# The cross terms of a complex filter product formed on VectorE, with one inverse matmul per class

## The chip, the cores and the metric

One Trainium2 chip, one of its eight NeuronCores. The metric is the device time of one execution of the whole program in microseconds (us), the median of the executions that were timed. A ratio of two kernels is computed as the mean time of one kernel's runs over that of the other's runs of the same rounds, so it is not quite the ratio of the medians that are quoted.

## The reference, cut to what matters

```python
def _attn_ref(x, filt_r, filt_i):            # x: 8 x 3008 x 256
    X = np.fft.rfft(x, axis=1)
    Y = X * (filt_r + 1j * filt_i)[None]     # complex product, one filter for all batches
    return np.fft.irfft(Y, n=x.shape[1], axis=1).astype(np.float32)

def _moe_ref(x, w_in, w_out, alpha):         # x: 24064 x 256, hidden width 2048
    h = x @ w_in
    s = np.sin(alpha * h)
    return ((h + s * s / (alpha + 1e-09)) @ w_out).astype(np.float32)
```

The kernel computes the Fourier transforms as matmuls in three stages per batch. Stage 1 is a 47-point transform. Stage 2 has 12 units of two frequency classes each: a forward matmul by the twiddle table, the product with the filter, and an inverse matmul. Stage 3 is the inverse 47-point transform. Between the stages the data go through DRAM to change the layout. The result feeds the "snake" layer: hidden matmuls (`ph`), a cosine on ScalarE, one VectorE instruction that makes `v`, and projection matmuls (`po`). The stages of the next batch are woven into the steps of the snake layer; one step is two hidden tiles and about eight projection matmuls, 48 steps are one batch.

## The kernel before

This is stage 2, as code. `xf` holds the spectrum with the real part in partitions 0 to 63 and the imaginary part in 64 to 127. `f_t[0]` and `f_t[1]` hold the real and the imaginary filter, each copied into both halves.

```python
        def stage2(u):
            if u < 12:
                ps = ...                                   # PSUM
                for i in range(2):
                    nc.tensor.matmul(out=ps[:, i, :], lhsT=d_t[:, s, :], rhs=..., ...)   # pb: forward
                xf = xfpool.tile([128, 2, C], FP16, ...)
                nc.scalar.copy(out=xf, in_=ps)
                for k in range(2):                         # two products of 128 x 512
                    nc.vector.tensor_tensor(out=pt, in0=xf, in1=f_t[k][:, 2 * u:2 * u + 2, :], op=ALU.mult)
            if u > 0:
                w = u - 1
                for i in range(2):
                    for k in range(2):                     # pc: two inverse matmuls per class add them up
                        nc.tensor.matmul(out=ps[:, i, :], lhsT=e_t[:, k, 2 * w + i, :],
                                         rhs=pr[k][:, i, :], start=(k == 0), stop=(k == 1))
                evac(st["g"][:, i0:i0 + 2, :], ps, ...)    # to g, then by DMA to DRAM (d2)
```

Because the second inverse matmul uses a table `e_t[:, 1]` with swapped and negated halves, TensorE forms the cross terms and their sum by accumulating in PSUM. The rest that the argument touches is the weaving:

```python
    def evac(dst, src, on_act=None):            # PSUM evacuations: every third on VectorE
        flip[0] = (flip[0] + 1) % 3
        ...
    hps = pool("hps", 4, PSUM)                  # four buffers for hidden tiles
    ...
    plan = {1: [-45 + i for i in range(8)],     # steps, counted from the first step that needs the batch
            2: [-29 + 14 * i / 13 for i in range(13)],
            3: [-10, -9] + [-7 + 2 * i for i in range(14)]}
```

Stage 2 therefore takes 14 of the 48 steps of a batch. The compiler's scheduler decides the exact order of each engine's instructions; the argument takes it that each engine keeps to that order at run time. TensorE's weight loads run beside its matmuls (544.2 and 799.8 us busy in a span of 837.2 us).

Of the kernel before, what the change touches and what calls it, by code (L numbers as in the profile page):

```python
# [9 lines left out]
FP16 = mybir.dt.float16  # L10
FP32 = mybir.dt.float32
AFT = mybir.ActivationFunctionType
ALU = mybir.AluOpType
# [3 lines left out]
B, S, C = 8, 3008, 256  # L17
DFF = 2048
N1, N2 = 47, 64
NS, NQ = 24, 64  # L20
# [34 lines left out]
def kernel(  # L55
# [10 lines left out]
    nc = tc.nc  # L66
# [17 lines left out]
    def pool(name, bufs, space=None):  # L84
        kw = {} if space is None else {"space": space}
        return ctx.enter_context(tc.tile_pool(name=name, bufs=bufs, **kw))
# [3 lines left out]
    t1pool = pool("t1", 4)  # L90
    t2pool = pool("t2", 4)
    xfpool = pool("xf", 3)
    ppool = pool("pp", 4)
    gpool = pool("gp", 4)
    t4pool = pool("t4", 3)
    opool = pool("op", 3)
# [3 lines left out]
    fps = pool("fps", 2, PSUM)  # L100
    hps = pool("hps", 4, PSUM)
    ops = pool("ops", 2, PSUM)
# [4 lines left out]
    d_t = cpool.tile([128, NS, 128], FP16)  # L107
    e_t = cpool.tile([128, 2, NS, 128], FP16)
    wi_t = cpool.tile([NK, NR], FP16)
    f_t = [cpool.tile([128, NS, C], FP16, name=f"filt{i}") for i in range(2)]  # L110

    marks = {}
# [17 lines left out]
    flip = [0]  # L130

    def evac(dst, src, on_act=None):
        flip[0] = (flip[0] + 1) % 3
        if flip[0] if on_act is None else on_act:
            marks["act"] = nc.scalar.copy(out=dst, in_=src)  # L135
        else:
            marks["dve"] = nc.vector.tensor_copy(out=dst, in_=src)  # L137

    def spectral(b):

        pieces = []
        d1 = dpool.tile([2 * NS, N2, C], FP16, name=f"d1_{b}", tag="d1")
        d2 = dpool.tile([2 * NS, N2, C], FP16, name=f"d2_{b}", tag="d2")
        d1_rows = d1.rearrange("a (h n) c -> (a h) n c", h=2)
        d2_rows = d2.rearrange("a (h n) c -> (a h) n c", h=2)
        st = {}

        def stage1(u):
            ch, half = divmod(u, 2)
            if u == 0:  # L150
                st["x"] = load_x(b)
            if half == 0:
                st["t1"] = t1pool.tile([NK, 8, C], FP16, name=f"t1_{b}_{ch}", tag="t1")
            for i in range(2):
                n0 = 4 * half + 2 * i
                ps = fps.tile([128, 512], FP32, name=f"pa_{b}_{u}_{i}", tag="f")
                marks["pe"] = nc.tensor.matmul(out=ps[0:NK, :], lhsT=wf_t, rhs=st["x"][ch][:, n0:n0 + 2, :],  # L157
                                               start=True, stop=True)
                evac(st["t1"][:, n0:n0 + 2, :], ps[0:NK, :])
            if half == 1:  # L160
                nc.sync.dma_start(out=d1_rows[:, 8 * ch:8 * ch + 8, :], in_=st["t1"])
            if u == 7:
                st["t2"] = []
                for g in range(4):
                    t2 = t2pool.tile([128, 6, C], FP16, name=f"t2_{b}_{g}", tag="t2")
                    for p in range(2):
                        a0 = p * NS + 6 * g
                        eng = nc.scalar if b == 0 and p else nc.sync
                        marks["t2", g] = eng.dma_start(out=t2[64 * p:64 * p + 64, :, :],
                                          in_=d1[a0:a0 + 6, :, :].rearrange("s n c -> n s c"))  # L170
                    st["t2"].append(t2)

        def stage2(u):
            if u < 12:

                ps = (ops if b == 0 else fps).tile([128, 2, C], FP32, name=f"pb_{b}_{u}",
                                                   tag="o" if b == 0 else "f")
                for i in range(2):
                    s = 2 * u + i
                    nc.tensor.matmul(out=ps[:, i, :], lhsT=d_t[:, s, :],  # L180
                                     rhs=st["t2"][s // 6][:, s % 6, :], start=True, stop=True)
                xf = xfpool.tile([128, 2, C], FP16, name=f"xf_{b}_{u}", tag="xf")
                nc.scalar.copy(out=xf, in_=ps)  # L183
                pr = []
                for k in range(2):
                    pt = ppool.tile([128, 2, C], FP16, name=f"p_{b}_{u}_{k}", tag="p")
                    marks["prod", u] = nc.vector.tensor_tensor(out=pt, in0=xf, in1=f_t[k][:, 2 * u:2 * u + 2, :],  # L187
                                                               op=ALU.mult)
                    pr.append(pt)
                st["p", u] = pr  # L190
            if u > 0:
                w = u - 1
                pr = st.pop(("p", w))
                if w % 3 == 0:
                    st["g"] = gpool.tile([128, 6, C], FP16, name=f"g_{b}_{w}", tag="g")
                ps = fps.tile([128, 2, C], FP32, name=f"pc_{b}_{w}", tag="f")
                for i in range(2):
                    for k in range(2):
                        nc.tensor.matmul(out=ps[:, i, :], lhsT=e_t[:, k, 2 * w + i, :],  # L199
                                         rhs=pr[k][:, i, :], start=(k == 0), stop=(k == 1))  # L200
                i0 = 2 * (w % 3)
                evac(st["g"][:, i0:i0 + 2, :], ps, i0 != 2 if b == 0 else None)
                if w % 3 == 2:
                    for p in range(2):
                        a0 = p * NS + 6 * (w // 3)
                        nc.sync.dma_start(out=d2[a0:a0 + 6, :, :].rearrange("s n c -> n s c"),
                                          in_=st["g"][64 * p:64 * p + 64, :, :])

        def stage3(u):
            ch, rest = divmod(u, 4)  # L210
            half, cb = divmod(rest, 2)
            if rest == 0:
                t4 = t4pool.tile([NK, 8, C], FP16, name=f"t4_{b}_{ch}", tag="t4")
                marks["t4"] = nc.sync.dma_start(out=t4, in_=d2_rows[:, 8 * ch:8 * ch + 8, :])
                st["t4"] = t4
            ps = fps.tile([128, 4, 128], FP32, name=f"pd_{b}_{u}", tag="f")
            psv = ps.rearrange("p a b -> p (a b)")[:, 0:4 * NR].rearrange("p (a r) -> p a r", r=NR)
            for i in range(4):
                nc.tensor.matmul(out=psv[:, i, :],  # L219
                                 lhsT=st["t4"][:, 4 * half + i, cb * 128:cb * 128 + 128],  # L220
                                 rhs=wi_t, start=True, stop=True)
            n0 = 8 * ch + 4 * half
            evac(y[:, cb, b % 2, n0:n0 + 4, :], psv)

        for u in range(8):
            pieces.append((1, lambda u=u: stage1(u)))
        for u in range(13):
            pieces.append((2, lambda u=u: stage2(u)))
        for u in range(16):
            pieces.append((3, lambda u=u: stage3(u)))  # L230
        return pieces
# [24 lines left out]
    for i in range(2):  # L256
        al_row.append(opool.tile([128, 2, C], FP32, name=f"al_row_{i}", tag="o"))
        for h in range(2):
            nc.scalar.dma_start(
                out=al_row[i][64 * h:64 * h + 1].rearrange("p a b -> p (a b)"),  # L260
# [3 lines left out]

    def dup_filter(g):
        gs = slice(6 * g, 6 * g + 6)
        for k in range(2):
            ins = nc.vector.tensor_copy(out=f_t[k][64:128, gs, :], in_=f_t[k][0:64, gs, :])
            behind(ins, marks["prod", 3 * g - 2] if g else s1_dve)

    for g in range(4):
# [9 lines left out]
    for g in range(3):  # L281
        pse = ops.tile([128, 8, 128], FP16, name=f"pse_{g}", tag="o")
        for i in range(8):
            behind(nc.tensor.transpose(out=pse[:, i, :], in_=d_t[:, 8 * g + i, :], identity=id16),
                   s1_pe)
        gs = slice(8 * g, 8 * g + 8)
        behind(nc.scalar.mul(e_t[:, 0, gs, :], pse, 0.125), s1_act)
        nc.vector.tensor_copy(out=e_t[0:64, 1, gs, :], in_=e_t[64:128, 0, gs, :])
        nc.vector.tensor_scalar(out=e_t[64:128, 1, gs, :], in0=e_t[0:64, 0, gs, :],
                                scalar1=-1.0, scalar2=None, op0=ALU.mult)  # L290

    ones = cpool.tile([128, 128], FP32)
    nc.vector.memset(ones, 2.0)
# [85 lines left out]
    def store(o_blk, pb, col):  # L379

        p = 0
        while p < 128:
# [11 lines left out]


    plan = {1: [-45 + i for i in range(8)],
            2: [-29 + 14 * i / 13 for i in range(13)],
            3: [-10, -9] + [-7 + 2 * i for i in range(14)]}
    pending = [(1 + i % 4 + 8 * (i // 4), 0, piece) for i, (_, piece) in enumerate(first[25:])]
    for b in range(1, B):  # L400
        at = {1: 0, 2: 0, 3: 0}
        for stage, piece in spectral(b):
            at_step = 48 * b + plan[stage][at[stage]]
            if b == 1 and stage < 3:
                at_step = 8 + at[stage] if stage == 1 else 23 + at[stage]
            at[stage] += 1
            pending.append((at_step, b, piece))
    pending.sort(key=lambda p: p[0])
# [46 lines left out]
```

## Time and profile before

| | before |
|---|---|
| time | 840.77 us, median of 3 (839.44 to 841.71) |
| TensorE (PE) busy | 96% |
| VectorE (DVE) busy | 75% |
| ScalarE (ACT) busy | 73% |
| GpSimd (POOL) busy | 3% |

The first part of the profile's page of the kernel before, the busy time of each engine in us, its share of the span and its instructions:

```profile
PE 799.8 (96%) x5793; PEld 544.2 (65%) x5793; DVE 628.1 (75%) x1119; ACT 613.0 (73%) x1200; POOL 28.3 (3%) x55
```

Two groups of instructions of the kernel before: line, engine, operation, output and inputs, shape, count, then busy us and mean ns of one, then the idle time of the engine ahead of them.

```profile
L187 DVE TENSOR_TENSOR p<-xf,filt 128x512 f16<-128x512 f16 x192 | 72.1, 419 | 4.9 <-ACT xf L183 4.5
...
L199 PE MATMUL pc<-p,e_t 128*128 128x256 f16 x384 | 59.7, 275 | 2.6 <-DVE p L187 1.5
```

Both means are latencies, not rates: instructions of one engine overlap. Rates are read from start to start. Here is stage 2 of batch 4 of the kernel before, first as busy time by stretch (us, busy us and instructions of PE, weight loads, DVE, ACT, POOL, then the granted clock of TensorE, the share of the DMA engines, and GB/s), then as VectorE's timeline (start, us, what, count, and the idle time ahead of it):

```profile
core 0: us, PE busy (x) PEld busy (x) DVE busy (x) ACT busy (x) POOL busy (x), PEclk, DMA share, GB/s
393.00:422.00 29.00, 28.95 (x214) 20.73 (x213) 25.27 (x52) 24.03 (x48) 0.00 (x0) 1.00 0.31 72
```

```profile
19.17 0.42 DVE L288 COPY e_t<-e_t 64x1024 f16<-64x1024 f16 x1
19.61 0.42 DVE L289 TENSOR_SCALAR e_t<-e_t 64x1024 f16<-64x1024 f16 x1
20.08 0.42 DVE L288 COPY e_t<-e_t 64x1024 f16<-64x1024 f16 x1
...
399.07 0.76 DVE L187 TENSOR_TENSOR p<-xf,filt 128x512 f16<-128x512 f16 x2
400.26 1.28 DVE L358 SCALAR_TENSOR_TENSOR v<-cos,ph 128x512 f16<-128x512 f32 x2 [0.43 <-ACT cos L357]
401.46 0.76 DVE L187 TENSOR_TENSOR p<-xf,filt 128x512 f16<-128x512 f16 x2
402.13 0.68 DVE L137 CAST g<-pc 128x512 f16<-128x512 f32 x1
402.73 1.28 DVE L358 SCALAR_TENSOR_TENSOR v<-cos,ph 128x512 f16<-128x512 f32 x2
```

What to see: TensorE has no gap in stage 2 (28.95 of 29 us), and VectorE has little room left (25.27 of 29). Two products take 0.75 us and one 0.42, so the second starts 0.335 us after the first. A snake instruction costs 0.60 (two take 1.28, one 0.68). The three lines at 19 to 20 us are set-up work whose input and output change partition halves from one instruction to the next: they start 0.44 and 0.47 us apart and do not overlap at all, though each lasts only 0.42.

### The profile page before, as it was taken

The numbers are of one execution on the slowest core, as the hardware profiler recorded it, in microseconds if no ns is written. First come the engines' busy times: TensorE is split into PE (matmuls) and PEld (weight loads), VectorE is DVE, ScalarE is ACT, GpSimd is POOL, SyncE is SP. The second block draws the span as 40 slices with busy tenths as digits, with TensorE's granted clock in tenths as the row PEclk, the third lists the DMA queues.
The fourth block names the chain that finished last, engine by engine and source line by source line (L and its number), as shares of the span: only waits on it lengthen the run. The fifth ranks groups of instructions, "written<-read, shape, count | busy, mean of one in ns | idle before, by whom it ended". The sixth has DMA issues, their size and how long they took to land.

```text
span 837.2 us, 16122 instructions
## 1 busy us (share of the span) xinstructions
PE 799.8 (96%) x5793; PEld 544.2 (65%) x5793; DVE 628.1 (75%) x1119; ACT 613.0 (73%) x1200; POOL 28.3 (3%) x55
## 2 busy tenths in 40 slices
PE   5758999999999999999999999999999999999996
PEld 2425676667776677666776677666777677666674
DVE  3658886778877788777877788777877778777772
ACT  4536886787868787787877777777877878677763
POOL 3210000000000000000000000000000000000000
PEclk9969999999999999999999999999999999999999
DMA  9985835185344744266242763447443353421111
GB/s 220 218 255 117 200 89 130 51 174 116 82 135 81 171 99 109 75 141 153 65 130 60 165 137 82 115 91 171 92 96 94 97 113 83 115 58 38 38 40 45
DMA packets 93495, 94.98 MB, mean 113 GB/s; under 512 B 8084, under 2 KB 82852, under 8 KB 93416
## 3 DMA queue, kind: packets, MB, share of 16 engines
q1 hardware_dynamic: 84784, 75.02, 34.5%
q0 software_dynamic: 6704, 18.09, 12.5%
q10 hardware_dynamic: 1928, 0.86, 0.5%
q8 instruction: 45, 0.74, 0.3%
q14 instruction: 34, 0.28, 0.1%
HBM read 58.02 MB, written 49.81 MB: 129 GB/s over the span
## 4 chain that ended last, share of the span: by engine, by line
PE 83%; DMA 7%; ACT 4%; issue 3%; DVE 2%; POOL 0%; SPq 0%; ACTq 0%; DVEq 0%; POOLq 0%
PE po L369 36%; PE ph L354 35%; PE pc L199 4%; PE pa L157 3%; ACT cos L357 2%; PE pd L219 2%; PE pb L180 2%; DMA t<-d 1%; DMA w_out<-in_moe_w_out_dram 1%; DMA d<-g 1%; DMA d_t<-d_tbl 1%; DVE p L187 1%; DMA x<-in_x_dram 1%; DMA filt<-in_filt_i_dram 1%; ACT t L135 1%
## 5 line engine op out<-in xcount | busy, mean ns | idle before, releaser
L358 DVE SCALAR_TENSOR_TENSOR v<-cos,ph 128x512 f16<-128x512 f32 (+1 forms) x768 | 484.0, 672 | 164.0 <-ACT cos L357 163.5
L357 ACT ACTIVATE cos<-ph 128x512 f32<-128x512 f32 (+1 forms) x768 | 411.6, 589 | 153.9 <-PE ph L354 152.5
L369 PE MATMUL po<-w,v 128*128 128x256 f16 x3008 | 400.9, 273 | 2.6 <-DVE w L337 2.6
L354 PE MATMUL ph<-y,w 128*128 128x512 f16 (+1 forms) x1536 | 391.5, 377 | 0.2 <-ACT y L135 0.2
L369 PEld LDWEIGHTS <-v 128*128 128x128 f16 x3008 | 289.0, 98 | 80.9 <-issue 8.7
L354 PEld LDWEIGHTS <-w 128*128 128x128 f16 x1536 | 150.4, 98 | 101.0 <-issue 4.6
L187 DVE TENSOR_TENSOR p<-xf,filt 128x512 f16<-128x512 f16 x192 | 72.1, 419 | 4.9 <-ACT xf L183 4.5
L375 ACT COPY o<-po 128x512 f32<-128x512 f32 x96 | 55.6, 579 | 17.7 <-PE po L369 15.5
L135 ACT CAST t<-pa 96x512 f16<-96x512 f32 x89 | 51.0, 589 | 19.0 <-PE pa L157 18.9
L183 ACT CAST xf<-pb 128x512 f16<-128x512 f32 x96 | 57.0, 595 | 8.1 <-PE pb L180 5.5
L219 PEld LDWEIGHTS <-t 96*128 96x128 f16 x512 | 36.3, 100 | 39.8 <-DMA t<-d 11.8
L199 PE MATMUL pc<-p,e_t 128*128 128x256 f16 x384 | 59.7, 275 | 2.6 <-DVE p L187 1.5
L157 PE MATMUL pa<-x,wf_t 94*96 94x512 f16 x128 | 47.2, 408 | 10.1 <-DMA x<-in_x_dram 6.3
L219 PE MATMUL pd<-wi_t,t 96*128 96x94 f16 x512 | 43.4, 208 | 11.1 <-DMA t<-d 10.9
L135 ACT CAST y<-pd 128x376 f16<-128x376 f32 x82 | 39.1, 479 | 12.5 <-PE pd L219 12.5
L199 PEld LDWEIGHTS <-e_t 128*128 128x128 f16 x384 | 37.6, 99 | 15.6 <-issue 7.1
L180 PE MATMUL pb<-t,d_t 128*128 128x256 f16 x192 | 38.2, 283 | 2.5 <-DMA t<-d 1.5
L135 ACT CAST g<-pc 128x512 f16<-128x512 f32 x64 | 38.7, 605 | 1.6 <-PE pc L199 1.6
L137 DVE CAST t<-pa 96x512 f16<-96x512 f32 x39 | 26.6, 683 | 15.8 <-PE pa L157 15.8
L180 PEld LDWEIGHTS <-d_t 128*128 128x128 f16 x192 | 18.9, 101 | 23.8 <-issue 4.6
L118 POOL DMA_DIRECT2D x<-in_x_dram x32 | 16.7, 524 | 502.8 <-PE pa L157 490.5
L157 PEld LDWEIGHTS <-wf_t 94*96 94x96 f16 x128 | 16.6, 129 | 19.6 <-issue 9.9
(28 smaller groups left out, 94.3 us busy)
## 6 DMA issues: line engine op xcount, KB each, us to landing
d<-t SPq DMA_DIRECT2D x32, 384.0 KB
d<-g SPq DMA_DIRECT2D x64, 192.0 KB
t<-d SPq DMA_DIRECT2D x32, 384.0 KB
x<-in_x_dram POOLq DMA_DIRECT2D x32, 376.0 KB, 6.9
t<-d SPq DMA_DIRECT2D x60, 192.0 KB
out_dram<-o SPq DMA_DIRECT2D x72, 94.0 KB
w_in<-in_moe_w_in_dram POOLq DMA_DIRECT2D x2, 1024.0 KB, 9.2
w_out<-in_moe_w_out_dram POOLq DMA_DIRECT2D x1, 2048.0 KB, 11.6
```

The lines of the kernel that those rows point to most:

```text
L135: marks["act"] = nc.scalar.copy(out=dst, in_=src)
L157: marks["pe"] = nc.tensor.matmul(out=ps[0:NK, :], lhsT=wf_t, rhs=st["x"][ch][:, n0:n0 + 2, :], start=True, stop=True)
L180: nc.tensor.matmul(out=ps[:, i, :], lhsT=d_t[:, s, :], rhs=st["t2"][s // 6][:, s % 6, :], start=True, stop=True)
L183: nc.scalar.copy(out=xf, in_=ps)
L187: marks["prod", u] = nc.vector.tensor_tensor(out=pt, in0=xf, in1=f_t[k][:, 2 * u:2 * u + 2, :], op=ALU.mult)
L199: nc.tensor.matmul(out=ps[:, i, :], lhsT=e_t[:, k, 2 * w + i, :], rhs=pr[k][:, i, :], start=(k == 0), stop=(k == 1))
L219: nc.tensor.matmul(out=psv[:, i, :], lhsT=st["t4"][:, 4 * half + i, cb * 128:cb * 128 + 128], rhs=wi_t, start=True, stop=True)
L354: nc.tensor.matmul(out=ps[:, 0:n], lhsT=w1[:, cb, jb * 128:jb * 128 + 128], rhs=y_cols[:, cb, c0:c0 + n], start=(cb == 0), stop=(cb == 1))
L357: nc.scalar.activation(out=cs[:, 0:n], in_=ps[:, 0:n], func=AFT.Sin, bias=float(np.pi / 2))
L358: marks["snake"] = nc.vector.scalar_tensor_tensor(out=v[k][:, jb, 0:n], in0=cs[:, 0:n], scalar=-1.0, in1=ps[:, 0:n], op0=ALU.add, op1=ALU. ...
L369: nc.tensor.matmul(out=pso[k][:, t % 2, :], lhsT=v[k][:, jb, 128 * t:128 * t + 128], rhs=w2[:, jb, :], start=(jb == 0), stop=(jb == 15))
L375: nc.scalar.copy(out=o[:, 0:nb, :], in_=pso[k][:, 0:nb, :])
```

## The change

The intent is to take matmuls off TensorE, which limits the kernel. From batch 1 on VectorE forms the cross terms itself: two half products read one partition half and write the other one, a full product gives the direct terms, and an add folds both into one tile ("the fold" from here on). One inverse matmul per class is then enough. The sign moves into the filter's upper half. Evacuations move from VectorE to ScalarE (one in five instead of one in three), and stage 2 gets a 14th piece, because the inverse matmul now comes one piece later.

```diff
-    ppool = pool("pp", 4)
+    ppool = pool("pp", 6)
...
-        flip[0] = (flip[0] + 1) % 3
+        flip[0] = (flip[0] + 1) % 5
...
+        lo, hi, every = slice(0, 64), slice(64, 128), slice(0, 128)
...
         def stage2(u):
             if u < 12:
+                forward(u)
+            if 0 <= u - 1 < 12:
+                new_products(u - 1)
+                prod(nc.vector, 1, u - 1, lo, hi)       # reads 0..63, writes 64..127
+                prod(nc.vector, 1, u - 1, hi, lo)       # reads 64..127, writes 0..63
+                prod(nc.vector, 0, u - 1, every, every)
+            w = u - 1
+            if 0 <= w < 12:
+                p0, p1 = st["p", w]
+                nc.vector.tensor_tensor(out=p0, in0=p0, in1=p1, op=ALU.add)
+                st["p", w].pop()
+            if 0 <= w - 1 < 12:
+                inverse(w - 1)                          # one matmul per class
...
-            2: [-29 + 14 * i / 13 for i in range(13)],
+            2: [-30 + 14 * i / 13 for i in range(14)],
```

Batch 0 keeps the old form (`stage2_first`, cut here, as are the filter's sign and the table's).

More of the change, by code (lines that the diff above doesn't have):

```diff
@@ L171, in stage1, with forward @@
                     st["t2"].append(t2)
+        def forward(u):
+            ps = (ops if b == 0 else fps).tile([128, 2, C], FP32, name=f"pb_{b}_{u}",
+                                               tag="o" if b == 0 else "f")
+            for i in range(2):
+                s = 2 * u + i
+                nc.tensor.matmul(out=ps[:, i, :], lhsT=d_t[:, s, :],
+                                 rhs=st["t2"][s // 6][:, s % 6, :], start=True, stop=True)
+            xf = xfpool.tile([128, 2, C], FP16, name=f"xf_{b}_{u}", tag="xf")
+            nc.scalar.copy(out=xf, in_=ps)
+            st["xf", u] = xf
@@ new lines, in inverse @@
+        def inverse(w):
+            pr = st.pop(("p", w))
+            if w % 3 == 0:
+                st["g"] = gpool.tile([128, 6, C], FP16, name=f"g_{b}_{w}", tag="g")
+            ps = fps.tile([128, 2, C], FP32, name=f"pc_{b}_{w}", tag="f")
+            for i in range(2):
+                for k, pt in enumerate(pr):
+                    nc.tensor.matmul(out=ps[:, i, :], lhsT=e_t[:, k, 2 * w + i, :],
+                                     rhs=pt[:, i, :], start=(k == 0), stop=(k == len(pr) - 1))
+            i0 = 2 * (w % 3)
+            evac(st["g"][:, i0:i0 + 2, :], ps, i0 != 2 if b == 0 else None)
+            if w % 3 == 2:
+                for p in range(2):
+                    a0 = p * NS + 6 * (w // 3)
+                    nc.sync.dma_start(out=d2[a0:a0 + 6, :, :].rearrange("s n c -> n s c"),
+                                      in_=st["g"][64 * p:64 * p + 64, :, :])
@@ new lines, in prod, with new_products, stage2_first @@
+        def prod(eng, k, u, rows, to):
+            marks["prod", u] = eng.tensor_tensor(out=st["p", u][k][to, :, :], in0=st["xf", u][rows, :, :],
+                                                 in1=f_t[k][rows, 2 * u:2 * u + 2, :], op=ALU.mult)
+        def new_products(u):
+            st["p", u] = [ppool.tile([128, 2, C], FP16, name=f"p_{b}_{u}_{k}", tag="p") for k in range(2)]
+        lo, hi, every = slice(0, 64), slice(64, 128), slice(0, 128)
+        def stage2_first(u):
+            if u < 12:
+                forward(u)
+                new_products(u)
+                for k in range(2):
+                    prod(nc.vector, k, u, every, every)
+            if u > 0:
+                inverse(u - 1)
@@ L173, in stage2 @@
         def stage2(u):
             if u < 12:
-                ps = (ops if b == 0 else fps).tile([128, 2, C], FP32, name=f"pb_{b}_{u}",
-                                                   tag="o" if b == 0 else "f")
-                for i in range(2):
-                    s = 2 * u + i
-                    nc.tensor.matmul(out=ps[:, i, :], lhsT=d_t[:, s, :],
-                                     rhs=st["t2"][s // 6][:, s % 6, :], start=True, stop=True)
-                xf = xfpool.tile([128, 2, C], FP16, name=f"xf_{b}_{u}", tag="xf")
@@ L183, in stage2 @@
-                nc.scalar.copy(out=xf, in_=ps)
-                pr = []
-                for k in range(2):
-                    pt = ppool.tile([128, 2, C], FP16, name=f"p_{b}_{u}_{k}", tag="p")
-                    marks["prod", u] = nc.vector.tensor_tensor(out=pt, in0=xf, in1=f_t[k][:, 2 * u:2 * u + 2, :],
-                                                               op=ALU.mult)
-                    pr.append(pt)
-                st["p", u] = pr
-            if u > 0:
-                w = u - 1
-                pr = st.pop(("p", w))
-                if w % 3 == 0:
-                    st["g"] = gpool.tile([128, 6, C], FP16, name=f"g_{b}_{w}", tag="g")
-                ps = fps.tile([128, 2, C], FP32, name=f"pc_{b}_{w}", tag="f")
-                for i in range(2):
-                    for k in range(2):
-                        nc.tensor.matmul(out=ps[:, i, :], lhsT=e_t[:, k, 2 * w + i, :],
-                                         rhs=pr[k][:, i, :], start=(k == 0), stop=(k == 1))
-                i0 = 2 * (w % 3)
-                evac(st["g"][:, i0:i0 + 2, :], ps, i0 != 2 if b == 0 else None)
-                if w % 3 == 2:
-                    for p in range(2):
-                        a0 = p * NS + 6 * (w // 3)
-                        nc.sync.dma_start(out=d2[a0:a0 + 6, :, :].rearrange("s n c -> n s c"),
-                                          in_=st["g"][64 * p:64 * p + 64, :, :])
@@ new lines, in stage2 @@
+                forward(u)
+            if 0 <= u - 1 < 12:
[10 more added lines that the diff above has]
+                inverse(w - 1)
@@ L226, in spectral @@
             pieces.append((1, lambda u=u: stage1(u)))
-        for u in range(13):
-            pieces.append((2, lambda u=u: stage2(u)))
+        for u in range(13 if b == 0 else 14):
+            pieces.append((2, lambda u=u: (stage2_first if b == 0 else stage2)(u)))
         for u in range(16):
@@ L266, in dup_filter @@
         gs = slice(6 * g, 6 * g + 6)
-        for k in range(2):
-            ins = nc.vector.tensor_copy(out=f_t[k][64:128, gs, :], in_=f_t[k][0:64, gs, :])
+        for ins in (nc.vector.tensor_copy(out=f_t[0][64:128, gs, :], in_=f_t[0][0:64, gs, :]),
+                    nc.vector.tensor_scalar(out=f_t[1][64:128, gs, :], in0=f_t[1][0:64, gs, :],
+                                            scalar1=-1.0, scalar2=None, op0=ALU.mult)):
             behind(ins, marks["prod", 3 * g - 2] if g else s1_dve)
@@ L288 @@
         nc.vector.tensor_copy(out=e_t[0:64, 1, gs, :], in_=e_t[64:128, 0, gs, :])
-        nc.vector.tensor_scalar(out=e_t[64:128, 1, gs, :], in0=e_t[0:64, 0, gs, :],
-                                scalar1=-1.0, scalar2=None, op0=ALU.mult)
+        nc.vector.tensor_copy(out=e_t[64:128, 1, gs, :], in_=e_t[0:64, 0, gs, :])
     ones = cpool.tile([128, 128], FP32)
@@ L404 @@
             if b == 1 and stage < 3:
-                at_step = 8 + at[stage] if stage == 1 else 23 + at[stage]
+                at_step = 8 + at[stage] if stage == 1 else 23 + 13 * at[stage] / 13
             at[stage] += 1
```

## The prediction

> **What bounds the kernel now.** TensorE. The page gives it 96% busy (799.8 of 837.2 us), and from about 80 us on it is busy 99.7 of every 100 us (busy time by stretch). VectorE is 75% and ScalarE 73% busy, but unevenly. In stage 2 of a later batch (392 to 422 us, by the timeline) one unit takes about 2.4 us of TensorE: four hidden matmuls, two forward, four inverse, eight projections. In the same stretch VectorE has idle gaps of only about 0.45 us per unit, and none where it also evacuates a `g` tile. So VectorE is already close to full there.
>
> **Removed.** Batches 1 to 7 lose 2 of 4 inverse matmuls in 12 units: 168 matmuls. Eight 256-column matmuls start 0.87 us after the eight before, so one costs 0.109 us (the group table's mean of 275 ns is latency). That is 168 x 0.109 = 18.3 us, all of it on the critical path: 2.2%. Alone it would give 822 us.
>
> **Added.** Per unit, VectorE goes from two 128x512 products to two half-partition products, one full product and one add. In the trace two products in a row take 0.75 us, one takes 0.42, so they start 0.335 apart. A half product has as many elements per partition, so it costs as much. The Trainium skill ("VectorE: DVE Perf Modes", section "Two Vector instructions with no wait between them") says that an instruction whose input or output starts in another partition quadrant than the last one's starts only when all earlier ones have finished. The trace agrees: the filter copy into the upper half starts after the product in front has ended, and the `e_t` copies (0.42 us each, alternating halves) start 0.44 us apart with no overlap. So each half product costs about 0.45 us, and the instruction ahead of the first loses its overlap of 0.1 us: 0.10 + 0.45 + 0.45 + 0.335 + 0.335 = 1.67 us per unit, against 0.67. The evacuations that move to ScalarE (1 in 5 instead of 1 in 3) give back 0.08.
>
> **On the critical path.** I counted the compiled instruction order. Between a batch's first product and last add VectorE has 48 products and adds, 25 to 27 snake operations (0.60 apart) and 2 or 3 evacuations: 36 to 38 us. TensorE's work for the same steps is 27 to 29 us. VectorE becomes the limit of stage 2, by about 9 us per batch, 63 us in seven. Lag can hide part: four hidden PSUM buffers and the later place of the inverse matmuls let TensorE lead by about a step, an estimated 2 us per batch, 14 in all. Net: 840.8 - 18.3 + 63 - 14 = 871; I take 869. Outside stage 2 nothing much changes; batch 0 is as before.
>
> **What would show it.** Product and add group: about 0.42 us each; half products without overlap. VectorE over 95% busy in each stage 2, no longer waiting for ScalarE there. TensorE busy about 80% there instead of 100%, its waits on PSUM freed by VectorE and on the add. Stage 2 about 36 us instead of 29. Inverse matmuls 216, not 384. Time outside stage 2 unchanged.
>
> **What would make it wrong.** If half products overlap (no hold), stage 2 needs 4 us less per batch, and the result is about 840. If buffers hide more of the lag, the loss shrinks. If TensorE's and VectorE's in-order waits interlock, it grows. Faster needs both no hold and nearly full hiding.
>
> Predicted 869 us, range 846 to 888; faster by over 2%: 0.04; within 2%: 0.15; slower by over 2%: 0.81.

## The result, and the profile after

The changed kernel takes 875.09 us, median of 4 (872.24 to 878.00), against 840.61 us for the kernel before in the same rounds: ratio 1.0411, 95% interval 1.0373 to 1.0448. It is slower by 4%, inside the predicted range of 846 to 888 and 6 us above the predicted 869. The profile is of the slowest of the four (878.0 us).

| | before | after |
|---|---|---|
| time, us | 840.61 | 875.09 |
| inverse matmuls | 384 | 216 |
| VectorE products and adds | 192 | 360 |
| span of a later batch's products and adds on VectorE, us | 27.3 to 29.1 | 36.6 to 38.2 |
| mean granted clock of TensorE | 0.988 | 0.979 |

Part 1 of the page of the changed kernel, and its groups that answer to those of before, shapes kept apart:

```profile
PE 802.2 (92%) x5625; PEld 526.1 (60%) x5625; DVE 673.6 (77%) x1242; ACT 638.0 (73%) x1245; POOL 28.1 (3%) x55
```

```profile
L203 DVE TENSOR_TENSOR p<-xf,filt 64x512 f16<-64x512 f16 x168 | 70.5, 420 | 4.4 <-ACT xf L182 0.5
...
L192 PE MATMUL pc<-p,e_t 128*128 128x256 f16 x216 | 42.1, 283 | 16.9 <-DVE p L233 12.2 <-DVE p L203 1.5 <-DVE g L137 1.1
...
L233 DVE TENSOR_TENSOR p<-p,p 128x512 f16<-128x512 f16 x84 | 35.2, 419 | 0.2
```

A half product takes 420 ns, the same as a full one. On average over the span VectorE looks harmless at 77%. The stretches tell more. Here are stage 2 of batch 4 and three slices of 2 us after the end of stage 2 of batch 2, in the columns as above:

```profile
core 0: us, PE busy (x) PEld busy (x) DVE busy (x) ACT busy (x) POOL busy (x), PEclk, DMA share, GB/s
408.00:446.00 38.00, 35.02 (x249) 23.20 (x247) 37.15 (x79) 28.81 (x56) 0.00 (x0) 1.00 0.34 79
...
248.00:250.00 2.00, 0.81 (x9) 0.76 (x10) 0.00 (x0) 0.27 (x1) 0.00 (x0) 0.54 0.71 191
250.00:252.00 2.00, 2.00 (x10) 1.13 (x8) 0.00 (x0) 1.62 (x4) 0.00 (x0) 0.50 0.04 14
252.00:254.00 2.00, 2.00 (x11) 1.34 (x10) 1.11 (x2) 0.52 (x2) 0.00 (x0) 0.50 0.20 46
```

In stage 2 VectorE is busy 37.15 of 38 us (98%), and TensorE is no longer full. The chain of waits of the changed kernel in that stretch (start, us, what the span was waiting for) runs over VectorE from 407.44 to 445.89, but for 3.3 us from 415.69 on, where it goes through TensorE's inverse matmuls and ScalarE's `xf` and back. Before the change the chain, read from 393 to 400 us, ran over TensorE alone. A piece of it before (first fence), then the chain after the change: its beginning, the detour, and what follows its end:

```profile
395.24 0.22 PE pb L180 x2
395.46 0.44 PE pc L199 x4
395.90 0.87 PE po L369 x8
396.77 0.86 PE ph L354 x4
```

```profile
407.44 1.28 DVE v L387 x2
408.75 0.42 DVE p L203
409.19 0.42 DVE p L203
409.62 0.42 DVE p L203
410.05 1.20 DVE v L387 x2
411.25 0.34 DVE p L233
...
415.69 0.39 PE pc L192 x2
...
418.39 0.60 ACT xf L182
419.00 1.28 DVE v L387 x2
...
451.47 4.83 DMA t<-d
456.30 0.04 issue
456.35 0.51 PE pd L248 x8
```

The two half products (408.75, 409.19) and the full one (409.62) start 0.43 to 0.44 us apart, as predicted, where two full products started 0.335 apart. The end of the chain is what I had not predicted: stage 3 (`pd`) waits for a DMA that brings in the result of stage 2. TensorE's waits, from 60 us on, as total us, times and the longest; before (first fence) and after (second):

```profile
PE pd L219 <- DMA t<-d: 1.6, 1, 1.6
```

```profile
PE pd L248 <- DMA t<-d: 15.2, 7, 3.8
PE pc L192 <- DVE p L233: 12.2, 36, 1.0
PE ph L383 <- DVE v L387: 4.9, 23, 0.3
```

After four of these seven waits the granted clock falls to half, three times for 3.4 us and once for 6.8, as the slices at 250 and 252 us show (10 and 11 matmuls in 2 us; before the change, 747 in the 100 us from 180 us on, so about 15 in 2 us).

To see where TensorE's time went I cut the steady part (from the first product of batch 1 to that of batch 7) into three kinds of stretch: from a batch's first product to its last product or add; from there to the first `pd` of stage 3; and the rest. "Work" is the matmuls begun in a stretch, each at its start-to-start interval as read from the traces (0.216 us for 512 columns, 0.162 for 384, 0.109 for 256, 0.042 for the 94 columns of `pd`); "unfilled" is the length minus the work, so matmuls at half clock count as partly unfilled. The traces hold all matmul records (5793 and 5625, 168 apart). All in us, six batches:

| kernel | stage 2: length, work, unfilled | to `pd`: length, work, unfilled | rest: length, work, unfilled | total length |
|---|---|---|---|---|
| before | 172.0, 167.5, 4.5 | 66.2, 63.9, 2.3 | 341.1, 335.4, 5.7 | 579.3 |
| after | 224.6, 194.6, 30.0 | 65.5, 51.0, 14.5 | 318.7, 304.1, 14.6 | 608.8 |

The unfilled time grows by 25.5 us within stage 2, by 12.3 before stage 3 and by 8.9 in the rest, where the half clock falls: 46.7 us. The work falls by 17.1 us: 144 matmuls x 0.109 = 15.7 us that the change takes out, and 1.4 that moved to outside these six batches. The difference is the growth of the total, 29.5 us.

### The profile page after: what moved, and what is told of

The parts are those of the page before. It is cut to its first block, busy times and chain, and to the rows that moved or that the text cites. A ratio compares the mean times of both kernels' runs of the same rounds, so it can differ in the third digit from the quotient of the medians.

```text
span 876.2 us, 15856 instructions
## 1 busy us (share of the span) xinstructions
PE 802.2 (92%) x5625; PEld 526.1 (60%) x5625; DVE 673.6 (77%) x1242; ACT 638.0 (73%) x1245; POOL 28.1 (3%) x55
## 3 DMA queue, kind: packets, MB, share of 16 engines
q0 software_dynamic: 6704, 18.09, 12.2%
## 4 chain that ended last, share of the span: by engine, by line
PE 48%; DVE 28%; DMA 11%; ACT 7%; issue 4%; SPq 1%; ACTq 0%; DVEq 0%; POOLq 0%
PE ph L383 22%; PE po L398 20%; DVE v L387 12%; DVE p L203 11%; DMA t<-d 6%; ACT cos L386 4%; DVE p L233 3%; PE pa L157 3%; PE pd L248 2%; ACT t L135 2%; DMA d<-t 2%; DMA w_out<-in_moe_w_out_dram 1%; DVE g L137 1%; DMA d<-g 1%; PE pc L192 1%
## 5 line engine op out<-in xcount | busy, mean ns | idle before, releaser
L386 ACT ACTIVATE cos<-ph 128x512 f32<-128x512 f32 (+1 forms) x768 | 418.2, 593 | 129.1 <-PE ph L383 124.7
L398 PE MATMUL po<-w,v 128*128 128x256 f16 x3008 | 414.8, 274 | 3.0 <-DVE w L366 3.0
L383 PE MATMUL ph<-y,w 128*128 128x512 f16 (+1 forms) x1536 | 407.9, 380 | 6.0 <-DVE v L387 4.9
L383 PEld LDWEIGHTS <-w 128*128 128x128 f16 x1536 | 151.1, 99 | 97.5 <-issue 14.4
L203 DVE TENSOR_TENSOR p<-xf,filt 64x512 f16<-64x512 f16 (+1 forms) x276 | 115.0, 421 | 11.0 <-ACT xf L182 5.4
L135 ACT CAST t<-pa 96x512 f16<-96x512 f32 x106 | 60.5, 598 | 15.0 <-PE pa L157 14.8
L135 ACT CAST y<-pd 128x376 f16<-128x376 f32 x99 | 46.8, 479 | 27.0 <-PE pd L248 27.0
L135 ACT CAST g<-pc 128x512 f16<-128x512 f32 x75 | 44.1, 588 | 24.9 <-PE pc L192 24.5
L192 PE MATMUL pc<-p,e_t 128*128 128x256 f16 x216 | 42.1, 283 | 16.9 <-DVE p L233 12.2
L192 PEld LDWEIGHTS <-e_t 128*128 128x128 f16 x216 | 16.9, 100 | 46.8 <-DVE p L233 38.3
L233 DVE TENSOR_TENSOR p<-p,p 128x512 f16<-128x512 f16 x84 | 35.2, 419 | 0.2
```

What stands on the lines that cost most here:

```text
L135: marks["act"] = nc.scalar.copy(out=dst, in_=src)
L203: marks["prod", u] = eng.tensor_tensor(out=st["p", u][k][to, :, :], in0=st["xf", u][rows, :, :], in1=f_t[k][rows, 2 * u:2 * u + 2, :], op= ...
L233: nc.vector.tensor_tensor(out=p0, in0=p0, in1=p1, op=ALU.add)
L383: nc.tensor.matmul(out=ps[:, 0:n], lhsT=w1[:, cb, jb * 128:jb * 128 + 128], rhs=y_cols[:, cb, c0:c0 + n], start=(cb == 0), stop=(cb == 1))
L386: nc.scalar.activation(out=cs[:, 0:n], in_=ps[:, 0:n], func=AFT.Sin, bias=float(np.pi / 2))
L398: nc.tensor.matmul(out=pso[k][:, t % 2, :], lhsT=v[k][:, jb, 128 * t:128 * t + 128], rhs=w2[:, jb, :], start=(jb == 0), stop=(jb == 15))
```

## The experiments

Theory: stage 2 became VectorE's, because of its four instructions per unit instead of two and because the changing halves take away their overlap. Rivals: TensorE's matmuls were worth nothing to begin with; ScalarE, which got more evacuations, is the limit; the new waits for stage 3's load are a loss of their own. Twelve kernels ran, with runs of the kernel before (medians 839.95 to 840.95 us).

### TensorE's part alone

```diff
-                    for k in range(2):
+                    for k in range(2 if b == 0 else 1):
```
(in the kernel before; the line with the `stop` flag, which follows suit, is cut; the result is wrong)

> The kernel before, with one inverse matmul per class from batch 1 on and the products left as they were (wrong result on purpose): TensorE's part of the change alone. Theory (before, TensorE is the limit everywhere, and 168 matmuls at 0.109 us are all on the path): 822 us, 18 us faster. Rival (VectorE or ScalarE already pace stage 2 before the change, so the matmuls are worth little): 836 to 841 us. Stage 2's products should span about 26 to 27 us a batch in place of 29.

Measured: 823.84 us against 840.57, ratio 0.9801 (0.9782 to 0.9819). The removal of 168 matmuls is worth 16.7 us of the estimated 18.3. The saving is real, and before the change TensorE was the limit. The products of a batch span 25.2 to 27.3 us.

### The inverse matmul put back, twice

```diff
-                st["p", w].pop()
+                st["p", w][1] = p0        # the sum goes through two inverse matmuls
```
(in the changed kernel; wrong result)

> The changed kernel with a second inverse matmul per class put back on TensorE (the sum multiplied twice, wrong result on purpose): VectorE's part of the change alone. Theory (VectorE needs 37 us for stage 2 of a batch, TensorE with the matmuls back about 31): the matmuls fit into TensorE's idle time, 875 us give or take 5, so that removing them in the change was worth next to nothing. Rival (TensorE's work still adds to the time): 875 + 18 = 893 us.

Measured: 890.03 us (ratio 1.0585). That is 15 us over the changed kernel, close to the rival's 893. My theory, in the form "TensorE has idle time in stage 2, so its matmuls are free", fell. The compiled order offered an excuse: in this kernel 28 of the 84 adds stood behind a half product on VectorE, against 7 in the changed kernel. So I forced the order in both forms: a unit's products behind the add of the unit ahead (the line that sets `marks["add"]` is cut).

```diff
+                for args in ((1, u - 1, lo, hi), (1, u - 1, hi, lo), (0, u - 1, every, every)):
+                    prod(nc.vector, *args)
+                    if u > 1:
+                        behind(marks["prod", u - 1], marks["add"])
```

> The changed kernel with a unit's products ordered behind the add of the unit before, so that VectorE's order no longer depends on what TensorE is thought to do (the run that put the inverse matmuls back had another order of products and adds on VectorE: its adds stood behind a half product 28 times instead of 7). This is the base for the next run: 868 to 878 us, products spanning 37 to 38 us a batch.

> The run before this one in the list, with the second inverse matmul per class put back on TensorE (wrong result on purpose). Theory (stage 2 is VectorE's time; the 15 us that the matmuls cost when they were first put back came mostly from a worse order on VectorE): 2 to 6 us over the base. Rival (the path goes through both engines in turn, so that TensorE's work adds whatever VectorE does): 12 to 18 us over the base.

Measured: 875.89 us for the base and 888.94 with the matmuls put back: 13 us more. The rival stands, the excuse does not (the two orders were still not alike: 19 adds stood right behind their product in the second, 5 in the first). The table of stretches shows why, with the same columns:

| kernel | stage 2 | to `pd` | rest | total length |
|---|---|---|---|---|
| forced order | 224.6, 195.7, 28.9 | 65.9, 50.5, 15.4 | 316.7, 303.5, 13.2 | 607.2 |
| forced order, matmul back | 226.2, 196.6, 29.6 | 70.0, 57.0, 13.0 | 322.5, 311.8, 10.7 | 618.7 |

Stage 2 is as long in both, within 2 us of 225, as VectorE dictates. TensorE's work in it is nearly the same too. What differs is which work. In the six stages 2 the base does 90.0 us of projections and 14.4 of inverse matmuls, the other one 77.6 and 28.8. Without the matmuls the scheduler had filled their place with projections, which else run after stage 2. So TensorE's saving is kept in this kernel, moved behind stage 2, and the unfilled time is not free room: in the order in which TensorE has to work, about 5 us per batch stay empty with or without the matmuls. That answer is worked out from counts in the traces; no run fixed TensorE's own order.

### Stage 2 three steps earlier

```diff
-    plan = {1: [-45 + i for i in range(8)],
-            2: [-30 + 14 * i / 13 for i in range(14)],
+    plan = {1: [-48 + i for i in range(8)],
+            2: [-33 + 14 * i / 13 for i in range(14)],
```

> The changed kernel with stages 1 and 2 of batches 2 to 7 placed 3 steps earlier, so that more hidden and projection work lies between the last inverse matmul and stage 3. If the waits of stage 3 for its loads (15 us in all) and the half clock behind them (about 8 us) are a loss of their own: 852 to 860 us. If they are only where VectorE's lag comes due, which TensorE would else wait for within stage 2: 872 to 878 us. The span of the products stays about 37 us a batch in both.

Measured: 854.65 us, correct, ratio to before 1.0170 (1.0153 to 1.0188): 20.4 us less than the changed kernel. The waits for stage 3's load are gone:

```profile
PE pd L248 <- DMA t<-d: 0.8, 2, 0.5
```

The mean clock is 0.988 as before the change. The stretch of the products did not move (36.5 to 38.2 us), and the unfilled time within stage 2 stayed (30.9 us in six batches), while on the way to `pd` 63.8 of 65.5 us are filled, against 51.0 of 65.5 in the changed kernel. So the waits and the half clock behind them were a loss of their own, about 20 us of the 51 that lie between the changed kernel and TensorE's part alone. It is an indirect one: VectorE ends stage 2 later, TensorE has by then done part of the projections that used to hide the way through DRAM, and nothing is left to do while the load is under way.

### No change of halves

```diff
-                prod(nc.vector, 1, u - 1, lo, hi)
-                prod(nc.vector, 1, u - 1, hi, lo)
+                prod(nc.vector, 1, u - 1, every, every)
+                nc.vector.tensor_tensor(out=spare[0], in0=st["xf", u - 1],
+                                        in1=f_t[1][:, 2 * u - 2:2 * u, :], op=ALU.mult)
```
(four full instructions per unit as in the change, none of which starts in another half; the line that makes the spare tile is cut; wrong result)

> The changed kernel with the two half products replaced by two full products that read and write from partition 0 (one of them into a spare tile; wrong result on purpose): the same number of VectorE instructions of the same elements per partition, and no instruction that starts in another quadrant than the one ahead. Theory (each change of the starting quadrant costs the overlap of about 0.11 us, three per unit): products start 0.335 us apart, the span of a batch's products falls from 37.4 to about 33.5 us, the time to 840 to 855 us. Rival (the count of instructions alone matters, not their halves): span 37 us, time 872 to 878.

Measured: 848.73 us (ratio 1.0086), 26.4 us less than the changed kernel, with as many VectorE instructions. The products span 33.0 to 34.2 us. VectorE's timeline of this run in stage 2 of batch 4:

```profile
407.08 1.28 DVE L389 SCALAR_TENSOR_TENSOR v<-cos,ph 128x512 f16<-128x512 f32 x2
408.28 0.42 DVE L229 TENSOR_TENSOR spare<-xf,filt 128x512 f16<-128x512 f16 x1
408.61 0.42 DVE L203 TENSOR_TENSOR p<-xf,filt 128x512 f16<-128x512 f16 x1
408.95 0.68 DVE L137 CAST g<-pc 128x512 f16<-128x512 f32 x1
```

The instructions last 0.42 us as ever, but start 0.33 us apart, and the first one starts 1.20 us after two snake instructions, not 1.31 (407.44 to 408.75 in the changed kernel). The unfilled time within stage 2 falls from 30.0 to 7.3 us, nearly to that of before, while that ahead of stage 3 (16.1) and in the rest (13.7) stays. The overlap that the changing halves take away is therefore nearly the whole direct loss within stage 2. Together, the two experiments account for 20.4 + 26.4 = 46.8 us over the 823.84 us of TensorE's part alone, so for 871 of the 875 us, if they add up; that is not shown, since no kernel had both.

### Evacuations shared as before

```diff
-        flip[0] = (flip[0] + 1) % 5
+        flip[0] = (flip[0] + 1) % 3
```

> The changed kernel with the evacuations shared as before, every third on VectorE instead of every fifth. Theory (VectorE is the limit of stage 2): one or two more evacuations of 0.6 us among a batch's products, 878 to 884 us. Rival (ScalarE, which got those evacuations, is the limit of stage 2 now): 865 to 872 us.

Measured: 874.15 us (872.66 to 876.55), no difference from the changed kernel. Both expectations missed. The products' stretches are longer, as I expected (266.6 us in seven batches against 261.9), but the remaining steps are shorter by about as much. ScalarE is not the limit of stage 2, and the shift of evacuations buys nothing.

### The full product on GpSimd

```diff
-                prod(nc.vector, 0, u - 1, every, every)
+                prod(nc.gpsimd, 0, u - 1, every, every)
```

> The changed kernel with the full product of each unit of batches 1 to 7 on GpSimd, idle 97% of the time. Theory: VectorE loses 0.335 us per unit, 4 us of 37 per batch; if GpSimd does a product within a unit's 2.4 us and does not slow VectorE, the time falls to 840 to 855 us. If the two engines hold each other up on their inputs, VectorE's instructions get longer than 0.42 and 0.68 us and the time stays at 870 or grows.

Measured: 871.19 us, correct, ratio 1.0375. Two groups of this run:

```profile
L203 POOL TENSOR_TENSOR p<-xf,filt 128x512 f16<-128x512 f16 x84 | 99.9, 1189 | 284.2 <-ACT xf L182 266.5 <-DVE p L203 12.5 <-DVE p L233 3.4
...
L203 DVE TENSOR_TENSOR p<-xf,filt 64x512 f16<-64x512 f16 x168 | 88.5, 527 | 4.8 <-ACT xf L182 0.3
```

GpSimd needs 1.19 us per product, which a unit has room for. But VectorE's half products grow from 420 to 527 ns, so 84 x 2 x 0.107 = 18 us go back of the 28 us (84 x 0.335) that leave VectorE, and TensorE waits for the add longer (24.8 us instead of 12.2). Its wait for stage 3's load is nearly gone here (0.6 us), so what this kernel loses, it loses in stage 2. The Trainium skill ("SBUF — State Buffer", section "Who interferes with whom") says that a VectorE instruction with two SBUF inputs contends with a GpSimd instruction that reads SBUF. This run agrees: the half products have two such inputs, and they got 25% longer. The 68 of them that ran beside a GpSimd product took 684 ns on average, 96 that did not 420; the snake instruction, with one input in SBUF and one in PSUM, took 0.68 us either way.

### Stage 2 spread out

The added VectorE work hurts because it is packed into 14 steps. So I spread the 14 pieces over 29 steps, with stage 1 earlier and stage 3 longer.

```diff
-    plan = {1: [-45 + i for i in range(8)],
-            2: [-30 + 14 * i / 13 for i in range(14)],
-            3: [-10, -9] + [-7 + 2 * i for i in range(14)]}
+    plan = {1: [-61 + i for i in range(8)],
+            2: [-46 + 29 * i / 13 for i in range(14)],
+            3: [-10, -9, -4, -3] + [2 * i for i in range(12)]}
```

> The changed kernel with the 14 pieces of stage 2 of batches 2 to 7 spread over 29 steps instead of 14 (stage 1 moved ahead, stage 3 spread to the same end plus 3 steps). Theory (the added VectorE work hurts only because it is packed into 14 of 48 steps; over a whole batch VectorE has about 83 us of work and TensorE about 95): TensorE is the limit again for six of seven batches, and its saving shows: 822 to 832 us, below both kernels. Rival (the longer chain of products, add and inverse, or the VectorE work itself, costs whatever its place): 850 or more.

Measured: 844.33 us, correct, ratio 1.0048 (1.0025 to 1.0071): 31 us better than the change, but 12 us or more above what I expected. Between the first products of batches 2 and 7 it takes 476.2 us, against 485.1 before and 473.9 in the run of TensorE's part alone, so there the saving shows. The loss is around batches 1 and 2, where TensorE is busy only 16 to 19 of every 20 us between 100 and 200 us. So I folded later, and gave batch 2 a narrower spread; then folded later still, with a control. Of each edit one line is shown; its other lines set the steps.

```diff
-            pieces.append((2, lambda u=u: (stage2_first if b == 0 else stage2)(u)))
+            pieces.append((2, lambda u=u: (stage2_first if b <= 1 else stage2)(u)))   # and 20 steps for batch 2
```

> The fold from batch 2 on only, batch 1 as before the change, and stage 2 of batch 2 spread over 20 steps, of batches 3 to 7 over 29. Theory: TensorE is the limit again, with 144 matmuls less (15.7 us), and the loss of the spread run around batch 1, where TensorE waited between 140 and 180 us, is gone: 824 to 833 us, faster than both kernels. Rival (the VectorE work costs about 4 us a batch even when spread): 838 or more.

```diff
+            pieces.append((2, lambda u=u: (stage2_first if b < 3 else stage2)(u)))    # and stage 1 from -64 on
```

> The fold from batch 3 on only; batches 1 and 2 in the form and at the steps of before; in batches 3 to 7 stage 2 spread over 29 steps, and stage 1 three steps earlier still than in the first spread run, because TensorE waited about 2 us for stage 2's first load in two batches there. Theory (with room, VectorE's added work is free and TensorE's saving shows): 120 matmuls at 0.109 us less, 13 us, so 826 to 833 us. Rival (the fold costs as much as it saves even when spread): 838 or more.

```diff
+            pieces.append((2, lambda u=u: (stage2_first)(u)))                         # the same steps, no fold: 13 pieces, so 27 of the 29 steps
```

> The same steps without any fold: every batch has two products and two inverse matmuls per class, as before. It tells whether a gain of the run ahead comes from the fold or from the spreading alone. Before is limited by TensorE 99.7% of the time in its steady part, so spreading alone should give nothing: 838 to 844 us. If it falls to 835 or less, the gain was the schedule's.

Measured, in turn: 840.16 us (ratio 0.9980, 0.9957 to 1.0003), 840.26 us (1.0016, 0.9996 to 1.0035), and 844.66 us for the control (1.0056, 1.0039 to 1.0074). All three are correct. None beats the kernel before, so my expectations for the first two both missed by 7 us or more, on the side of their rivals, and the control came out just above its range. Against the control the fold is worth 4.4 us, little above the scatter (839.8 to 845.0 us against 842.9 to 847.3), where 120 matmuls were estimated at 13. In the settled batches it does show: from batch 4 to batch 7 the first products are 284.1 us apart with the fold and 291.0 without, 2.3 us per batch of the possible 2.6. The first spread batch gives it back: from its first product to that of batch 4 it takes 101.7 us with the fold and 98.2 without. TensorE waits for stage 3's loads again, once each in batches 1, 2 and 3; from 60 us on:

```profile
PE pd L248 <- DMA t<-d: 8.7, 3, 4.1
```

(2.7 us in the control, in one wait, in batch 1.) Whether steps tuned batch by batch would reach about 830 us is left open.

## Why the prediction was right

It was right in the direction, the time and the cause, with two sizes wrong that nearly cancel. That they cancel is luck, and with it the small miss of 6 us.

- TensorE is the limit before, and the matmuls are on the path: right. Predicted 18.3 us, measured 16.7 with them alone removed. (The 99.7 of every 100 us hold from 180 us on; from 80 to 180 us the trace has 97.84.)
- VectorE's cost per unit, with 0.45 us per half product and the lost overlap: right. Predicted 36 to 38 us for a batch's stretch, measured 36.6 to 38.2. The Trainium skill ("VectorE: DVE Perf Modes", section "Two Vector instructions with no wait between them") gave the rule that an instruction that starts in another quadrant waits for all earlier ones; the run without the change of halves shows what it costs, 26.4 us of time. The prediction named this as what would make it wrong if absent, and put the result without it at about 840; it was 849.
- "VectorE becomes the limit of stage 2, by about 9 us per batch", of which "an estimated 2 us per batch" hidden: the term was mis-sized. The unfilled time of TensorE in stage 2 grew by 25.5 / 6 = 4.2 us per batch, not 7, because the scheduler pulled projections and hidden matmuls into the stretch (work of 194.6 instead of 167.5 us in six batches, with 2.6 us per batch of matmuls gone). The prediction took TensorE's work there as fixed at 27 to 29 us; it was 32.
- "Outside stage 2 nothing much changes": wrong. Waits for stage 3's load and the half clock behind them cost about 20 us (the run with stage 2 three steps earlier). This makes up for the term ahead: 4.2 us per batch within stage 2 and (12.3 + 8.9) / 6 = 3.5 outside it come to 7.8 us per batch, where 7 were predicted.
- TensorE busy "about 80%" in stage 2: wrong, 35.02 of 38 us, 92%. VectorE "over 95%": right, 98%, and its waits for ScalarE there (3.6 us in stage 2 of batch 4 before) are gone, as predicted. TensorE's waits for the add and for PSUM freed by VectorE: there, but small (12.2 and 4.9 us), since projections fill in.
- The evacuations that move to ScalarE "give back 0.08" per unit: not seen; undoing that part changes nothing (874.15 against 875.09 us).

## What to carry to other kernels

Read an engine's load in the stretch where the added work lands, not over the span: VectorE at 75% had 25.27 of 29 us taken in stage 2, and four instructions per unit did not fit. Count a VectorE instruction by its start-to-start time, and count one that changes partition halves at its full latency. When a stage gets longer, ask also what its end releases: here a large part of the loss was a load that the longer stage pushed out of the shadow of other work, and moving the stage three steps earlier gave 20 us back without touching the arithmetic.

## What the Trainium skill lacked or had wrong

- "VectorE: DVE Perf Modes", section "Two Vector instructions with no wait between them", tells when an instruction is held but not what that costs. Here a held 512-element fp16 product starts 0.43 us after the product ahead of it instead of 0.335, and a snake instruction in front of a held one loses 0.11 us of overlap; without the three holds in each of 84 units the kernel took 26.4 us less.
- "TensorE: Matmul & The Clock Gate", section "Part 1: The HAM clock gate", puts the half rate after at least one idle window of about 3.4 us. In the changed kernel four of seven waits were followed by a clock of 0.50 (512-column matmuls started 0.427 us apart, not 0.216), and three of these showed only 2.1, 2.7 and 2.3 us of idle time in the trace; a wait of 2.4 us elsewhere was not followed by it. The place of a wait counts, not its length alone: the four half-clock stretches begin 31, 91 and 151 times 3.413 us after the first, and in the 3.41 us ahead of each TensorE was idle for 2.8, 2.1, 1.9 and 2.0 us. The other three waits leave at most 1.5 us of idle time in any piece of that grid. In the other runs' traces, from 80 to 825 us, the pieces with half clock behind them have 1.9 us or more and the others at most 1.8, but for one of 1.98 (forced order). A wait well below 3.4 us can thus cost more than its own length: about 1.7 us more for 3.4 us at half clock, by estimate.
- "SBUF — State Buffer", section "Who interferes with whom", names the contention of GpSimd and a two-input VectorE instruction but no size for this mix: half products of 420 ns became 527 ns on average over all, and 684 ns for those beside a GpSimd product of 1.19 us.
